# Loads of v split over two DMA queues: partitions 64 to 127 from ScalarE, 0 to 63 from SyncE

## The chip, the cores and the metric

The kernel runs on one core of a Trainium2 chip. The metric is the device time of one execution in microseconds; 225.95 us is the median of three runs of the kernel before. The engines are TensorE (PE, with PEld for its weight loads), VectorE (DVE), ScalarE (ACT), GpSimd (POOL) and SyncE (SP). [...] SP does no arithmetic here; it issues DMAs. [...]

## What is computed

x is 2048 x 512 in bfloat16. It is normalized per row; the result xn feeds two branches, which are multiplied and added to x:

```python
xn = _layernorm(x, axis=-1)
s = _A_ref(xn, A_wqkv, A_wo)          # local dilated attention, 32 heads of 16
g = _silu(_B_ref(xn, B_w_gate, B_w_up, B_w_down))   # (gelu(xn@w_gate) * (xn@w_up)) @ w_down
return x + s * g
```

In the attention, position i sees the eight positions i, i-2, ..., i-14 (W = 8, dilation 2):

```python
idx = pos[:, None] - off[None, :]     # off = 0, 2, ..., 14
kg = k[:, :, idx_c, :].reshape(B, H, S, W, Dh)
vg = v[:, :, idx_c, :].reshape(B, H, S, W, Dh)
logits = jnp.einsum("bhsd,bhswd->bhsw", q, kg) * scale
attn = _softmax(jnp.where(mask, logits, -1e9), axis=-1)
o = jnp.einsum("bhsw,bhswd->bhsd", attn, vg)
```

## The kernel before

The 2048 positions are worked in four blocks of 512 (j = 0 to 3). For each block TensorE does, in this order: 14 GLU steps (`glu`: four matmuls for g_ps with w_gate, four for u_ps with w_up, L261), then the q, k and v projections of the next block (`qkv`, L261), then `down` for four tiles of 128 positions (14 matmuls each into y_ps, L477), with `sums` after the first of them, then `divide` and four times `finish` (four matmuls into s_ps, L493). The last block has no next one, and its `sums` stands at GLU step 12. All these PSUM tiles (g_ps, u_ps, qkv_ps, y_ps, s_ps, the softmax denominators and, for j > 0, the logits) rotate through one pool of four banks, `mm`; a tile waits until the one four before it has been read. In a GLU step ScalarE reads both banks: Gelu of g_ps to ge (L465), a copy of u_ps to u (L467). VectorE multiplies them to h (L469); ge and u have three buffers each.

The attention lies mostly on VectorE, in a layout in which partition 32 w + h holds head h at window offset w modulo 4. `qk_products` multiplies q with shifted k (pk, L332), TensorE sums over the head dimension into L_ps (L352), ScalarE takes the exponential E (L360). `av_product` (L404) and `av_pair` (L420, L428) multiply E with v_arr, TensorE sums into o_ps (L440), and `divide` multiplies with the reciprocal denominators rb into oT (L452), which s_ps reads.

v_arr has 128 partitions x 16 x 520 elements: four groups of 32 partitions, one per window offset wl = 0 to 3, each a shifted copy of the same v. The shift is made by a trip through DRAM: the projected v goes from vst to the DRAM tile vT (L290), and `load_v` (L306) reads it four times with offsets 2 apart, one DMA of 520 KB for each wl. v_arr has a single buffer, shared (tag "va") with pk4, the products of the upper four window positions of the next block: v of block j + 1 can be loaded only when the logits of j + 1 have been read from pk4.

The schedule is written out by hand: `at(key, fn)` hangs a function before a numbered step, `run` calls it there. Every DMA of the kernel before is issued from SP, in program order. At GLU step 0 of block 0 the order on SP is: one transpose of xn (L253), four loads of v, three more transposes, then w_down (L116), w_o (L119) and the rest of x (L88). For the later blocks `sums(j)` ends with: exponentials of block j + 1 on ScalarE; the reciprocals stored to DRAM (rs_d, L389) and read back spread over the partitions (rb, four DMAs, L395), then the four loads of v for j + 1. The one instruction that waits for v on the compute side is the first av_product of a block: GLU step 9 of block 0, GLU step 0 of the others.

On ScalarE the two exponentials in `sums` stand between two table loads: to Exp before (L533), back to Silu (L485) after them for the remaining y_ps tiles.

Of the kernel before, what the change touches and what calls it, by code (L numbers as in the profile page):

```python
# [18 lines left out]
WL = 4  # L19
# [9 lines left out]
def kernel(  # L29
# [13 lines left out]
    nc = tc.nc  # L43
# [225 lines left out]
    st = [dict(pk={}, pv={}, vst={}) for _ in range(NJ)]  # L269
# [27 lines left out]
        project(ps[:, 0, :], wqkv_sb, fo * P, j)  # L297
        copy_out(j, fo, ps[:])

    def load_v(j, wls=range(WL)):  # L300

        if wls[0] == 0:
            st[j]["va"] = vap.tile([P, DH, VW], BF16, name="v_arr", tag="va")
        va = st[j]["va"]
        for wl in wls:
            nc.sync.dma_start(  # L306
                out=va[H * wl : H * (wl + 1), :, :],
                in_=bass.AP(
                    tensor=vT.tensor,
                    offset=PAD + j * TQ - WL * DIL - DIL * wl,  # L310
                    ap=[[SV * DH, H], [SV, DH], [1, VW]],
                ),
            )
# [25 lines left out]
    def logits(j):  # L339
        if j == 0:  # L340
            nc.scalar.preload_act_table(AF.Exp)
            quad = att.tile([P, NC, TQ], F32, name="L_ps", tag="quad")
            L = [quad[:, wh, :] for wh in range(WH)]
        else:
            L = [mm.tile([P, TQ], F32, name="L_ps", tag="mm")[:] for _ in range(WH)]

        Eb = st[j]["Eb"] = ep.tile([P, WH, TQ], BF16, name="E")
        E = st[j]["E"] = Eb[:, ::-1, :]
        for wh in range(WH):
            for c in range(NC):  # L350
                for wl in range(WL):
                    nc.tensor.matmul(  # L352
                        L[wh][H * wl : H * (wl + 1), :],
                        lhsT=dsum[:, c, :],
                        rhs=st[j]["pk"][WL * wh + wl][:, c, :],
                        start=(c == 0),
                        stop=(c == NC - 1),
                    )
        for wh in range(WH):
            nc.scalar.activation(out=E[:, wh, :], in_=L[wh], func=AF.Exp, scale=SCALE)  # L360
        if j == 0:
            for w in range(1, W):
                wh, wl = divmod(w, WL)
                nc.gpsimd.memset(E[H * wl : H * (wl + 1), wh, 0 : w * DIL], 0.0)

    def denominators(j):

        E = st[j]["E"]
        den = mm.tile([P, P], F32, name="den_ps", tag="mm")
        for wh in range(WH):  # L370
            for q in range(4):
                nc.tensor.matmul(  # L372
                    den[H * q : H * (q + 1), :],
                    lhsT=hsum[:],
                    rhs=E[:, wh, q * P : (q + 1) * P],
                    start=(wh == 0),
                    stop=(wh == WH - 1),
                )
        st[j]["den"] = den

    def reciprocals(j):
        den = st[j]["den"]
        rs = sm2.tile([P, P], BF16, name="rs")
        with nc.allow_low_precision(reason="as the softmax of the reference"):
            nc.vector.reciprocal(out=rs[:], in_=den[:])
        st[j]["rs"] = rs

    def store_reciprocals(j):
        nc.sync.dma_start(out=rs_d[j][:, :], in_=st[j]["rs"][:])  # L389

    def spread_reciprocals(j):

        rb = op.tile([P, TQ], BF16, name="rb")
        for i in range(WL):
            nc.sync.dma_start(  # L395
                out=rb[H * i : H * (i + 1), :].rearrange("h (q i) -> h q i", q=4),
                in_=rs_d[j].rearrange("(q h) i -> h q i", h=H),
            )
        st[j]["rb"] = rb
# [32 lines left out]
    def av_sums(j):  # L432

        o = att.tile([P, NC, TQ], F32, name="o_ps", tag="quad")
        for g in range(NC):
            pv = st[j]["pv"]
            pvs = [pv[g]] if g in pv else [pv[g, wh] for wh in range(WH)]
            for n, p in enumerate(pvs):
                for i in range(4):
                    nc.tensor.matmul(  # L440
                        o[H * i : H * (i + 1), g, :],
                        lhsT=hsum[:],
                        rhs=p[:, i, :],
                        start=(n == 0),
                        stop=(n == len(pvs) - 1),
                    )
        st[j]["o"] = o
# [61 lines left out]
    def at(key, fn, *args):  # L509
        side.setdefault(key, []).append((fn, args))  # L510
# [19 lines left out]
    def sums(j):  # L530

        if j + 1 < NJ:
            nc.scalar.preload_act_table(AF.Exp)  # L533
        denominators(j)
        av_sums(j)
        if j + 1 < NJ:
            logits(j + 1)
        reciprocals(j)
        store_reciprocals(j)
        spread_reciprocals(j)  # L540
        if j + 1 < NJ:
            load_v(j + 1)

    for j in range(1, NJ):
        at(("qkv", j, 2), k_halo, j)
# [9 lines left out]
        for i, fc in enumerate(whole):  # L555
            at(("glu", j, fc), av_product, j, npair + i // 2, i % 2)
    at(("glu", NJ - 1, 12), sums, NJ - 1)


# [70 lines left out]
    for n, fo in enumerate((0, 2, 4, 6, 8, 10)):  # L630
# [5 lines left out]
                project(ps[:, i, i0 : i0 + w], wqkv_sb, (fo + i) * P, 0, HQ + i0, w)  # L636
        copy_out(0, fo, ps[:], HQ, HQ, 2)
    at(("glu", 0, 0), transpose_by_dma, TPQ)
    at(("glu", 0, 0), load_v, 0)
    for t in range(TPQ + 1, 2 * TPQ):  # L640
        at(("glu", 0, 0), transpose_by_dma, t)
    at(("glu", 0, 0), load_late_weights)
# [2 lines left out]
    for j in range(NJ):  # L645
        for fc in range(NF):
            run("glu", j, fc)
            glu(j, fc)
        if j + 1 < NJ:

            for i, fo in enumerate((0, 1, 4, 5, 2, 3, 6, 7, 8, 9, 10, 11)):
                run("qkv", j + 1, i)
                qkv(j + 1, fo)
            full = slice(0, D)
            sl = []
            for tt in range(TPQ):
                run("down", j, tt)
                sl.append(down(j, tt, full))
                if tt == 0:
                    sums(j)  # L660
            divide(j)
            for tt in range(TPQ):
                finish(j, tt, full, sl[tt])
        else:
            full, half = slice(0, D), (slice(0, D - P), slice(D - P, D))
            sl = [down(j, tt, full) for tt in range(TPQ - 1)]
            divide(j)
            finish(j, 0, full, sl[0])
            finish(j, 1, full, sl[1])
            finish(j, 2, full, sl[2])  # L670
            sl3 = down(j, 3, half[0])
            finish(j, 3, half[0], sl3)
            sl3 = down(j, 3, half[1])
            finish(j, 3, half[1], sl3)
# [28 lines left out]
```

The softmax here doesn't subtract the row's maximum and nothing guards it: scores larger than these inputs give would overflow.

## Time and profile before

| | |
|---|---|
| median of three runs | 225.95 us (225.94 to 226.25) |
| the profiled execution | 226.18 us |
| its span, first to last instruction | 224.5 us |
| mean granted TensorE clock | 0.999 |
| v_arr loads: issues, length of an issue, issue to landing | 16, 552 / 626 / 746 ns (min, median, max), 5.4 / 8.5 / 12.8 us |
| rb loads: issues, issue to landing | 16, 1.6 / 1.9 / 3.4 us |
| transposes of xn: issues, length of an issue, issue to landing | 12, 1188 / 1286 / 3444 ns, 2.4 / 4.2 / 12.5 us |
| data moved by DMA | 24.89 MB |

How to read it: busy time is the time in which an engine executes; issuing a DMA isn't counted as busy. A wait is idle time of an engine, put down to what released it. SPq rows in the timeline are DMA issues of SP, with the length of the issue, not of the transfer; a row with x4 holds four issues in a row. Matmul ends are modelled, so neighbouring groups overlap by some 0.15 us in the timeline. Some matmul records are missing from the trace.

### The profile page before, as it was taken

To read this page: it belongs to the slowest core of one execution; us is meant where nothing else is said; L and a number is where in the kernel's file an instruction comes from. 1 tells how busy PE (TensorE), PEld (TensorE's weight loads), DVE (VectorE), ACT (ScalarE), POOL (GpSimd) and SP (SyncE) were. 2 spreads that over 40 slices of the span, in tenths; PEclk is the share of its full clock that TensorE was granted. 3 is DMA by queue.
4 is the path that set the end of the run, shared out by engine and by line. 5 is a ranking of instruction groups with operands and counts; after the bars stand their busy time and mean duration, and the time that the engine had idled before them with its cause. 6 is when DMAs were issued, how large, how long until landed. Compare 5 with 4: busy or idle time off the path is not lost.

```text
span 224.5 us, 3548 instructions
## 1 busy us (share of the span) xinstructions
PE 219.3 (98%) x1293; PEld 106.0 (47%) x1314; DVE 172.9 (77%) x295; ACT 130.8 (58%) x207; POOL 21.6 (10%) x67
## 2 busy tenths in 40 slices
PE   8999999999999999999999999999999999999994
PEld 4994444444444444444444444444444444444443
DVE  4688963999984799989984799998944389982452
ACT  4386779667631767676752386767763177666211
POOL 1025981000120000000040000000000000000000
PEclk9999999999999999999999999999999999999999
DMA  6999799972079910000219960000117960001002
GB/s 207 376 402 260 148 198 146 359 212 96 12 152 199 213 23 0 0 3 1 93 41 210 187 164 0 3 0 0 67 41 151 197 147 0 0 0 28 6 23 70
DMA packets 30258, 24.89 MB, mean 111 GB/s; under 512 B 11040, under 2 KB 29728, under 8 KB 30240
## 3 DMA queue, kind: packets, MB, share of 16 engines
q1 hardware_dynamic: 30240, 24.66, 47.1%
q8 instruction: 10, 0.16, 0.3%
q14 instruction: 8, 0.07, 0.1%
HBM read 18.74 MB, written 4.34 MB: 103 GB/s over the span
## 4 chain that ended last, share of the span: by engine, by line
PE 96%; ACT 1%; issue 1%; DVE 0%; ACTq 0%
PE u_ps L261 22%; PE y_ps L477 22%; PE g_ps L261 20%; PE qkv_ps L261 16%; PE s_ps L493 6%; PE L_ps L352 3%; PE o_ps L440 3%; PE qk_ps L576 2%; ACT u L467 1%; PE warm_ps L244 1%; PE v_ps L576 1%; PE qk_ps L567 1%; PE den_ps L372 0%; PE v_ps L567 0%; PE trb L220 0%
## 5 line engine op out<-in xcount | busy, mean ns | idle before, releaser
L261 PE MATMUL u_ps<-xnT,wu_sb 128*128 128x512 bf16 x221 | 57.3, 379 | 0.4
L261 PE MATMUL g_ps<-xnT,wg_sb 128*128 128x512 bf16 x217 | 56.3, 379 | 0.1
L477 PE MATMUL y_ps<-wd_sb,h 128*128 128x512 bf16 (+2 forms) x234 | 49.5, 366 | 0.2
L467 ACT ACTIVATE u<-u_ps 128x512 bf16<-128x512 f32 x56 | 33.5, 599 | 14.8 <-PE u_ps L261 14.8
L465 ACT ACTIVATE ge<-g_ps 128x512 bf16<-128x512 f32 x56 | 33.5, 598 | 11.9 <-PE g_ps L261 8.9
L332 DVE TENSOR_TENSOR pk<-q_sb,k_sb 128x1024 bf16<-128x1024 bf16 (+1 forms) x56 | 38.9, 761 | 1.7 <-ACT k_sb L285 1.7
L261 PE MATMUL qkv_ps<-xnT,wqkv_sb 128*128 128x512 bf16 (+2 forms) x197 | 36.8, 344 | 0.2
L477 PEld LDWEIGHTS <-h 128*128 128x128 bf16 x238 | 22.6, 98 | 26.5 <-issue 1.3
L261 PEld LDWEIGHTS <-wu_sb 128*128 128x128 bf16 x224 | 21.9, 98 | 26.4
L261 PEld LDWEIGHTS <-wg_sb 128*128 128x128 bf16 x224 | 21.7, 98 | 26.6 <-issue 0.8
L404 DVE TENSOR_TENSOR pv<-E,v_arr 128x2048 bf16<-128x2048 bf16 x22 | 26.7, 1220 | 7.4 <-DMA v_arr<-vT 7.4
L485 ACT ACTIVATE sl<-y_ps 128x512 bf16<-128x512 f32 (+2 forms) x17 | 9.7, 572 | 32.7 <-PE y_ps L477 31.6
L469 DVE TENSOR_TENSOR h<-ge,u 128x512 bf16<-128x512 bf16 x56 | 23.1, 419 | 5.9 <-ACT u L467 5.8
L261 PEld LDWEIGHTS <-wqkv_sb 128*128 128x128 bf16 x200 | 18.9, 98 | 17.4
L501 DVE TENSOR_TENSOR m<-s_ps,sl 128x512 bf16<-128x512 f32 (+2 forms) x17 | 11.1, 655 | 18.4 <-PE s_ps L493 13.5
L420 DVE TENSOR_TENSOR two<-E,v_arr 128x1024 f32<-128x1024 bf16 x20 | 24.4, 1218 | 0.0
L204 POOL TENSOR_TENSOR rstd<-rstd,mhalf 128x1 f32<-128x1 f32 x12 | 7.0, 583 | 90.3 <-DVE rstd L201 90.3
L452 DVE TENSOR_TENSOR oT<-o_ps,rb 128x1024 bf16<-128x1024 f32 x8 | 9.4, 1217 | 7.7 <-DMA rb<-rs_d 7.7
L493 PE MATMUL s_ps<-wo_sb,oT 128*128 128x512 bf16 (+2 forms) x64 | 14.6, 366 | 0.2
L428 DVE TENSOR_TENSOR pv<-two 128x512 bf16<-128x512 f32 x20 | 13.8, 692 | 0.7
L465 ACT ACT_TABLE_LOAD x4 | 5.1, 1283 | 11.3 <-PE g_ps L261 11.3
L285 ACT ACTIVATE vst<-qkv_ps 128x512 bf16<-128x512 f32 x14 | 8.4, 597 | 3.7 <-PE qkv_ps L261 3.7
(65 smaller groups left out, 145.2 us busy)
## 6 DMA issues: line engine op xcount, KB each, us to landing
v_arr<-vT SPq DMA_DIRECT2D x16, 520.0 KB, 8.5
vT<-vst SPq DMA_DIRECT2D x8, 256.0 KB, 2.4
out_dram<-o_t SPq DMA_DIRECT2D x15, 128.0 KB, 3.4
wg_sb<-in_B_w_gate_dram SPq DMA_DIRECT2D x2, 896.0 KB, 9.9
wu_sb<-in_B_w_up_dram SPq DMA_DIRECT2D x2, 896.0 KB, 11.2
wd_sb<-in_B_w_down_dram SPq DMA_DIRECT2D x1, 1792.0 KB, 11.6
wqkv_sb<-in_A_wqkv_dram SPq DMA_DIRECT2D x4, 384.0 KB, 4.4
x_sb<-in_A_x_dram SPq DMA_DIRECT2D x3, 512.0 KB, 7.8
```

Source lines behind the costliest of these rows:

```text
L261: nc.tensor.matmul(ps, lhsT=w[:, dk, lo : lo + P], rhs=xnT[j][:, dk, i0 : i0 + n], start=(dk == 0), stop=(dk == NC - 1),)
L332: nc.vector.tensor_tensor(out=st[j]["pk"][w][:, c0 : c0 + n, :], in0=st[j]["q"][:, c0 : c0 + n, :], in1=k_sb[j][:, c0 : c0 + n, off : off ...
L404: nc.vector.tensor_tensor(out=pv[:], in0=st[j]["E"][:, wh, :].unsqueeze(1).to_broadcast([P, 4, TQ]), in1=st[j]["va"][:, 4 * g : 4 * g + 4, ...
L420: nc.vector.tensor_tensor(out=two[:], in0=st[j]["Eb"][:], in1=bass.AP(tensor=v.tensor, offset=v.offset, ap=[v.ap[0], [WL * DIL, WH], [1, T ...
L428: nc.vector.tensor_tensor(out=st[j]["pv"][g][:, d, :], in0=two[:, 0, :], in1=two[:, 1, :], op=ALU.add)
L465: nc.scalar.activation(out=ge[:], in_=g_ps[:], func=AF.Gelu_apprx_tanh)
L467: nc.scalar.activation(out=u[:], in_=u_ps[:], func=AF.Copy)
L469: nc.vector.tensor_tensor(out=h[:], in0=ge[:], in1=u[:], op=ALU.mult)
L477: nc.tensor.matmul(y[:], lhsT=st[j][fc][:, tt * P : (tt + 1) * P], rhs=wd_sb[:, fc, cols], start=(fc == 0), stop=(fc == NF - 1),)
L485: nc.scalar.activation(out=sl[:], in_=y[:], func=AF.Silu)
L493: nc.tensor.matmul(s[:], lhsT=st[j]["oT"][:, g, tt * P : (tt + 1) * P], rhs=wo_sb[:, g, cols], start=(g == 0), stop=(g == NC - 1),)
L501: nc.vector.tensor_tensor(out=m[:], in0=s[:], in1=sl[:], op=ALU.mult)
```

## The change

`load_v` takes the groups wl and the queue from its caller. In `sums` the groups 0 and 1 (partitions 0 to 63) are issued from SP as before, behind rb; the groups 2 and 3 (64 to 127) from ScalarE, where they stand behind the two exponentials and ahead of the Silu table load. For block 0 the groups 0 and 1 stay at GLU step 0 on SP, between the first transpose and the other three; the groups 2 and 3 are issued from ScalarE at GLU step 4, behind the u copy of step 3 and ahead of the Gelu of step 4. The order of all other instructions on every engine is kept. The first av_product of a block waits for all four loads, as before.

```diff
-    def load_v(j, wls=range(WL)):
-
-        if wls[0] == 0:
+    def load_v(j, wls, queue):
+
+        if "va" not in st[j]:
             st[j]["va"] = vap.tile([P, DH, VW], BF16, name="v_arr", tag="va")
         va = st[j]["va"]
         for wl in wls:
-            nc.sync.dma_start(
+            queue.dma_start(
                 out=va[H * wl : H * (wl + 1), :, :],
...
         if j + 1 < NJ:
-            load_v(j + 1)
+
+            load_v(j + 1, (0, 1), nc.sync)
+            load_v(j + 1, (2, 3), nc.scalar)
...
     at(("glu", 0, 0), transpose_by_dma, TPQ)
-    at(("glu", 0, 0), load_v, 0)
+    at(("glu", 0, 0), load_v, 0, (0, 1), nc.sync)
+    at(("glu", 0, 4), load_v, 0, (2, 3), nc.scalar)
     for t in range(TPQ + 1, 2 * TPQ):
         at(("glu", 0, 0), transpose_by_dma, t)
```

## The prediction

> **What bounds the kernel now.** I read the page's busy times first, then its chain, then the waits of all engines, then the timeline where v is loaded. Busy times and the chain's share by engine:
>
> ```profile
> PE 219.3 (98%) x1293; PEld 106.0 (47%) x1314; DVE 172.9 (77%) x295; ACT 130.8 (58%) x207; POOL 21.6 (10%) x67
> ...
> PE 96%; ACT 1%; issue 1%; DVE 0%; ACTq 0%
> ```
>
> TensorE is busy 219.3 of 224.5 us and makes up 96% of the chain. A share over the whole span can hide gaps, so I cut the run at its stage borders (each row: the stretch, its length, then busy time of PE, PEld, DVE, ACT, POOL, then clock, DMA share, GB/s):
>
> ```profile
> 17.10:53.40 36.30, 36.09 (x189) 16.26 (x191) 30.32 (x46) 27.10 (x44) 14.35 (x47) 1.00 0.96 202
> 53.40:72.90 19.50, 19.25 (x143) 8.80 (x145) 15.15 (x32) 8.03 (x10) 2.63 (x5) 1.00 0.63 131
> 72.90:126.30 53.40, 53.14 (x293) 24.13 (x296) 46.05 (x78) 32.28 (x50) 2.63 (x5) 1.00 0.36 72
> 126.30:179.70 53.40, 53.14 (x293) 24.13 (x296) 41.06 (x62) 32.29 (x50) 0.00 (x0) 1.00 0.36 75
> 179.70:221.40 41.70, 41.45 (x235) 19.61 (x237) 28.31 (x43) 21.48 (x35) 0.00 (x0) 1.00 0.13 33
> ```
>
> From 17.10 to 221.40 TensorE is idle for 0.21 + 0.25 + 0.26 + 0.26 + 0.25 = 1.23 us of 204.3. The waits that carry v and its neighbour rb are real, but they are VectorE's (total, times, longest):
>
> ```profile
> DVE oT L452 <- DMA rb<-rs_d: 7.7, 3, 5.3
> DVE pv L404 <- DMA v_arr<-vT: 7.4, 4, 3.7
> ```
>
> VectorE's 7.4 us for v leave no hole on TensorE: they are absorbed. Even the chain's 1% ACT (u L467) is no wait: at 27.30 the timeline shows three of a g_ps group's four matmuls, so one record is missing and the chain steps aside; the groups keep their 0.86 us spacing.
>
> Stage 0, where the first v is loaded (start, length, what):
>
> ```profile
> 22.57 2.71 SPq L306 DMA_DIRECT2D v_arr<-vT  x4
> ...
> 24.11 0.60 ACT L467 ACTIVATE u<-u_ps 128x512 bf16<-128x512 f32 x1 [0.33 <-PE u_ps L261]
> ...
> 24.91 0.60 ACT L465 ACTIVATE ge<-g_ps 128x512 bf16<-128x512 f32 x1 [0.21 <-PE g_ps L261]
> ...
> 25.33 8.57 SPq L253 DMA_TRANSPOSE xnT<-xn  x3
> ```
>
> And the same place for j = 1, after the second softmax:
>
> ```profile
> 60.34 0.60 ACT L360 ACTIVATE E<-L_ps 128x512 bf16<-128x512 f32 x1 [0.22 <-PE L_ps L352]
> 60.40 1.75 SPq L395 DMA_DIRECT2D rb<-rs_d  x4
> ...
> 60.95 1.28 ACT L485 ACT_TABLE_LOAD   x1
> ...
> 62.31 2.65 SPq L306 DMA_DIRECT2D v_arr<-vT  x4
> ...
> 63.45 0.60 ACT L485 ACTIVATE sl<-y_ps 128x512 bf16<-128x512 f32 x1 [1.21 <-PE y_ps L477]
> ...
> 64.08 2.35 DVE L452 TENSOR_TENSOR oT<-o_ps,rb 128x1024 bf16<-128x1024 f32 x2
> ...
> 69.30 3.62 PE L493 MATMUL s_ps<-wo_sb,oT 128*128 128x512 bf16 x15
> ```
>
> The reader should see ScalarE with 1.21 us to spare before its next y_ps, and oT ready at 66.43, 2.87 us before s_ps needs it.
>
> [...] from 64 to 69 us, while v lands, the DMA share is 1.05 at 208 GB/s, so the engines, not the queue, are full. [...] three transposes behind v took 8.57 us, three at 75.17 took 3.81.
>
> **The change, part by part.** Eight of 16 v loads leave SP, 0.626 us each (median of the L306 rows), so 1.25 us per stage. The same eight go to ScalarE, two per stage.
>
> *Stage 0.* The two issues come after u of GLU step 3 (ends 24.71). Behind them wait ge and u of step 4, and thus h(4) on VectorE. TensorE wants the PSUM bank that ge(4) frees (four banks, two per step) for g of step 6 at 27.30. ge takes 0.60, so the two issues may take 27.30 - 0.60 - 24.71 = 2.0 us for nothing. On SP the two loads that stay end near 22.57 + 1.35 = 23.9, and the three transposes, whose inputs are long there, follow at once instead of at 25.33: they meet ScalarE's issues. [...] 0.5 left of the first transpose (23.95 + 1.27 = 25.22), 0.63 for the first v, 1.27 for the second transpose, 0.63 for the second v: 3.0 us, to 27.75. ge(4) ends at 28.35, 1.05 us after 27.30, and TensorE stands for these 1.05 us. Bounds: 1.1 us (2 x 0.552, no waiting; less still if ScalarE issues while u runs), which costs 0; and each issue behind a transpose as slow as those behind four v loads (2.86): 2 x 2.86 + 1.25 = 7.0, a stall of 5.0. I take 3.0: [...] with two loads outstanding rather than four the transposes should take their quiet length. The delay isn't paid twice: u(4) ends at 28.95, its bank is wanted at 28.17 + 1.05, and ScalarE recovers, using 1.20 of each 1.73 us. On VectorE, which was ahead with pk, pk of w = 7 ends near 33.3 instead of 31.49; the logits that read it start at 32.6 + 1.05 and take the w below 4 first. Hidden.
>
> *v for stage 0.* The half on ScalarE starts 1 to 3 us later than now, and SP's transposes and w_down can overtake it. 2.1 MB at 190 to 200 GB/s still needs about 11 us, so v is complete near 37, as now (pv at 37.54). It may be 3.3 us late: h(9) ends 39.11, 1.56 before ge(12) at 40.67, which ends 1.79 before its bank is wanted at 43.06. I take 0; at 4 us late it would be 0.7.
>
> *Stages 1 to 3.* The issues stand after the second E (ends 60.94) and before the Silu table load. Queued behind: table load, three sl. Cost 1.25 us, 2.5 with turns, against 1.21 us of idle before sl: sl starts up to 1.3 us late. Its bank is wanted again only by the second s_ps, past 69.3: nothing. The waits attached are v stores and old loads, all landed (stores issued by 54.6, landing 2.4). All four loads are in flight by about 63.6 rather than 64.96: v at most 1.3 us earlier, so pv's waits (1.50, 1.26, 0.93 us for j = 1, 2, 3) shrink, worth 0. The next transpose is also issued 1.25 us earlier, beside v; should v end 1 us later instead, h(0) slips and ge(3) behind it, but ge(3) (78.99 to 79.59) frees a bank wanted at 81.4: nothing.
>
> *rb.* v stood behind rb; now two v loads enter beside rb's second to fourth. Slack of oT before s_ps: 2.87 (69.30 - 66.43), 2.58 (122.72 - 120.14), 3.26 us (176.15 - 172.89). Delay, low end 0. High end: two issues of 0.63 between rb's issues, 1.25; and three rb loads of 128 rows over 16 engines = 24 rows per engine, each behind one v row (1040 B at 190 GB/s / 16 = 88 ns), 2.1; together 3.4, so 0.5 + 0.8 + 0.1 = 1.4 us of stall in all. I take half of both, 1.7: hidden.
>
> *Start and end.* No v load stands before 22 us or after 172, so head and tail stay. [...]
>
> Sum: 1.05, all from stage 0. The profiled execution took 226.18 us, 1.68 around its span of 224.5, so its like would take 227.2; it lies 0.23 above the median of the runs, 225.95, against which the sum gives 227.0. Since turns can fall a little kinder (ScalarE may issue before u has ended), I say 226.9.
>
> **Rivals.**
> *N, not slower: the issues overlap.* Place: the same two issues of stage 0. If they take 0.63 to 1.0 each beside SP's transposes, ge(4) ends by 27.3 and TensorE never sees them: 226.0. It decides up to 2.0 us for both. For it: four v issues in a row took 0.68 each in this very traffic[...]. Against: [...] SP issuing at just that time. Chance 0.36.
> *A2, worse: the transposes stay slow* and hold ScalarE behind them: 5 to 7 us, a stall of 3 to 5, 229 to 231. For it: 2.86 us each now. Against: half the v loads ahead. 0.09.
> *B, rb comes late in the three later stages,* with or without stage 0's stall: 1.4 at the high end, 227.4. For it: v goes in beside rb, and rb's four issues took 2.66 for j = 2 on their own. Against: all of both parts must add. 0.08.
> *C, faster: v sooner lets VectorE run ahead.* If 7.4 us were on the path it would be 218.5, but TensorE's idle from 17 us on is 1.23 in all. Half of that: 225.3. 0.04.
> *D, the split does nothing for v,* [...] True or not, TensorE doesn't wait for v; the cases above stand.
> *E, a cost around the span or one not listed:* 226.6, 0.04.
>
> **How the numbers follow.** Forecast 0.39, N 0.36, A2 0.09, B 0.08, C 0.04, E 0.04. A measurement here can tell 0.2%, 0.45 us. Faster 0.04, same 0.36, slower 0.60. The forecast's own range is 226.4 to 228.0 (issues of 2.5 to 4 us). N pulls the low end to 225.7; at 228.6 A2 is left out above: 225.7 to 228.6.
>
> **What would show it.** Right: ScalarE's v issues of stage 0 last over 1 us, a hole on TensorE before g of step 6, the time otherwise stage for stage as before, pv's waits for v shorter with no gain. N: those issues at 0.63, PE idle still 0.2 to 0.3 in each stretch. B: s_ps waiting for oT. Wrong altogether: any time below 225.5, or a hole elsewhere.

## The result, and the profile after

| | before | after |
|---|---|---|
| median (lowest to highest) | 226.12 us, 6 runs on the same chip | 239.15 us (238.57 to 241.44), 6 runs |
| ratio, 95% interval | | 1.0586 (1.0536 to 1.0636) |
| profiled execution, its span | 226.18, 224.5 us | 240.8, 239.1 us |
| mean granted TensorE clock in it | 0.999 | 0.979 |

The change costs 13 us. The forecast was 226.9, and no rival went above 231. Here and below medians are over all runs of a kernel, ratios over those within 1.5% of its fastest. First the page of the kernel after: busy times, the granted clock in 40 slices, the two DMA queues (packets, MB, share of 16 engines; q1 is SP's, q10 ScalarE's) and the shares of the engines in the chain of work that ended last.

```profile
PE 225.5 (94%) x1293; PEld 106.6 (45%) x1314; DVE 173.5 (73%) x295; ACT 130.3 (54%) x207; POOL 20.9 (9%) x67
...
PEclk9999999999997999999999799999999989999999
...
q1 hardware_dynamic: 26016, 20.40, 34.3%
q10 hardware_dynamic: 4224, 4.26, 9.4%
...
PE 55%; DVE 21%; DMA 14%; issue 4%; SPq 2%; ACT 1%; ACTq 0%; DVEq 0%
```

The second queue is real: q10 moves 4.26 MB, eight loads of 0.53 MB. TensorE made up 96% of the chain; it makes up 55% now, and 14% are DMA. Such a share says where to look and not how much is lost: in a later experiment (e1) it is 41% and the loss is under 1 us. The clock has three dips that were not there. TensorE is also 6.2 us longer busy with the same 1293 matmuls, as a lower clock would make it.

Next the same stretches that the prediction cut out (length, then busy PE, PEld, DVE, ACT, POOL, then clock, DMA share, GB/s):

```profile
17.10:53.40 36.30, 36.09 (x189) 16.21 (x191) 28.11 (x42) 26.67 (x44) 13.70 (x47) 1.00 0.96 202
53.40:72.90 19.50, 16.91 (x129) 7.30 (x129) 14.96 (x31) 8.03 (x10) 2.63 (x5) 1.00 0.67 138
```

The first stretch holds the stage where the prediction put its whole loss. PE is busy 36.09 us in it, as before. The loss begins in the second, around 70 us. Where GLU starts tells the rest: blocks 1, 2 and 3 began at 72.75, 126.17 and 179.60; they begin at 78.54, 136.44 and 194.21. So 5.8, 4.5 and 4.3 us are lost between GLU of one block and GLU of the next, 14.6 in all, the whole difference of the two spans (the profiled execution is 1.65 us above the median). After 194.21 nothing is lost.

The waits of all engines that carry it (total, times, longest):

```profile
DVE oT L452 <- DMA rb<-rs_d: 21.8, 4, 10.6
...
DVE pv L404 <- DMA v_arr<-vT: 5.9, 1, 5.9
...
PE s_ps L493 <- DVE oT L452: 4.9, 6, 1.5
...
PE s_ps L493 <- DVE m L501: 2.6, 3, 0.9
```

VectorE waits 21.8 us for rb instead of 7.7, and the wait is now passed on: TensorE stands before s_ps for oT, twice in each of the three blocks, and three times for m, the product of s_ps and sl (Silu of y_ps) on VectorE (L501), which no s_ps did before. The timeline of the end of block 0 shows it in order (start, length, what; in brackets the idle time and what ended it):

```profile
61.13 0.33 SPq L389 DMA_DIRECT2D rs_d<-rs  x1
...
61.21 1.24 ACTq L306 DMA_DIRECT2D v_arr<-vT  x2
...
62.60 1.81 SPq L395 DMA_DIRECT2D rb<-rs_d  x4
...
70.63 2.35 DVE L452 TENSOR_TENSOR oT<-o_ps,rb 128x1024 bf16<-128x1024 f32 x2 [4.26 <-DMA rb<-rs_d]
71.91 0.60 PE L493 MATMUL s_ps<-wo_sb,oT 128*128 128x512 bf16 x2 [1.53 <-DVE oT L452]
73.05 0.60 PE L493 MATMUL s_ps<-wo_sb,oT 128*128 128x512 bf16 x2 [0.53 <-DVE oT L452]
...
74.50 2.29 PE L493 MATMUL s_ps<-wo_sb,oT 128*128 128x512 bf16 x5 [0.85 <-DVE m L501]
```

From the store of rs (the reciprocals) to the first load of rb, which reads it back, SP needs 1.5 us, since the store must have landed (1.4 to 1.6 us). ScalarE has nothing of the kind to wait for and issues its two v loads into that gap. What was behind rb in the program is ahead of it now. All four rb loads of this block land 6.5 to 7.0 us after their issue (before: 1.6 to 1.9).

The 5.8 us of this block can be added up. y_ps ends at 70.38, 1.1 later than the s_ps of before began (69.30): mostly a backlog from further up, treated below (the part of y_ps behind the sums began at 61.16 instead of 60.22). Then 1.53 and 0.53 for oT, 0.85 for m, and the rest, 1.8, is slow matmuls. That is read from the weight loads that go with them (same columns):

```profile
74.89 0.15 PEld L493 LDWEIGHTS <-oT 128*128 128x128 bf16 x1 [0.28 <-issue]
75.31 0.15 PEld L493 LDWEIGHTS <-oT 128*128 128x128 bf16 x1 [0.28 <-issue]
75.74 0.15 PEld L493 LDWEIGHTS <-oT 128*128 128x128 bf16 x1 [0.28 <-issue]
```

They start 0.42 us apart, where 0.215 is usual in this kernel (four matmuls of a group in 0.86). The granted clock is 0.50 from 74.06 to 77.47 us, and 1.00 just before and after.

What lands how late depends on what was issued ahead, and block 2 shows it singly. The issues, and then two narrow stretches of them (ns per issue, first and last start; us from issue to landing):

```profile
177.18 1.81 SPq L395 DMA_DIRECT2D rb<-rs_d  x4
...
177.69 1.23 ACTq L306 DMA_DIRECT2D v_arr<-vT  x2
```

```profile
L395 SPq DMA_DIRECT2D rb<-rs_d x1: 423/423/423, 177.6 to 177.6; - x1
...
DMA to landing us min/median/max: 1.7/1.7/1.7
```

```profile
L395 SPq DMA_DIRECT2D rb<-rs_d x2: 428/455/482, 178.0 to 178.5; - x2
...
DMA to landing us min/median/max: 4.4/5.9/7.4
```

ScalarE's two v loads start at 177.7 and 178.3. The rb loads issued ahead of both (177.2, 177.6) land after 1.6 and 1.7 us, the one between them (178.0) after 4.4, the one behind both (178.5) after 7.4. So each v load issued ahead adds 2.7 to 3.0 us. 0.53 MB at the 200 GB/s of this traffic (201 from 62.6 to 66.6 us in block 0) takes 2.7: rb lands as if the v loads ahead of it were moved first.

What the queues moved shows how strictly that holds (packets, MB, share of 16 engines). In block 0, from 62.6 to 66.6 us, with all four rb loads issued by 64.4, and in block 2, from 179.0 to 181.0:

```profile
q10 hardware_dynamic: 789, 0.80, 102.9%
```

```profile
q10 hardware_dynamic: 373, 0.39, 84.1%
q1 hardware_dynamic: 140, 0.03, 8.3%
```

In block 0 SP's queue moves nothing for 4 us while v is moved. In block 2 most of the rb load between the two v loads goes through among the packets of the first v, and only its last few packets come late. oT needs the whole of it, so the landing counts.

### The profile page after: what moved, and what is told of

Same layout as the page of the kernel before. It is cut to its first block, busy times and chain, and to the rows that moved or that the text cites. A ratio compares the mean times of both kernels' runs of the same rounds, so it can differ in the third digit from the quotient of the medians.

```text
span 239.1 us, 3551 instructions
## 1 busy us (share of the span) xinstructions
PE 225.5 (94%) x1293; PEld 106.6 (45%) x1314; DVE 173.5 (73%) x295; ACT 130.3 (54%) x207; POOL 20.9 (9%) x67
## 3 DMA queue, kind: packets, MB, share of 16 engines
q10 hardware_dynamic: 4224, 4.26, 9.4%
## 4 chain that ended last, share of the span: by engine, by line
PE 55%; DVE 21%; DMA 14%; issue 4%; SPq 2%; ACT 1%; ACTq 0%; DVEq 0%
PE u_ps L261 17%; PE g_ps L261 15%; DVE pk L332 12%; PE s_ps L493 7%; DMA rb<-rs_d 6%; DMA v_arr<-vT 6%; PE qkv_ps L261 5%; PE y_ps L477 5%; DVE pv L404 3%; DVE oT L452 3%; DMA rs_d<-rs 2%; SPq L395 2%; PE qk_ps L578 1%; DVE rs L385 1%; DVE m L501 1%
## 5 line engine op out<-in xcount | busy, mean ns | idle before, releaser
L493 PE MATMUL s_ps<-wo_sb,oT 128*128 128x512 bf16 (+2 forms) x64 | 19.8, 443 | 8.2 <-DVE oT L452 4.9
L452 DVE TENSOR_TENSOR oT<-o_ps,rb 128x1024 bf16<-128x1024 f32 x8 | 9.4, 1219 | 21.8 <-DMA rb<-rs_d 21.8
L501 DVE TENSOR_TENSOR m<-s_ps,sl 128x512 bf16<-128x512 f32 (+2 forms) x17 | 11.2, 657 | 14.8 <-PE s_ps L493 9.6
L493 PEld LDWEIGHTS <-oT 128*128 128x128 bf16 x68 | 7.1, 114 | 20.4 <-issue 9.7
## 6 DMA issues: line engine op xcount, KB each, us to landing
wd_sb<-in_B_w_down_dram SPq DMA_DIRECT2D x1, 1792.0 KB, 17.8
```

What stands on the lines that cost most here:

```text
L452: nc.vector.tensor_tensor(out=oT[:, g : g + 2, :], in0=st[j]["o"][:, g : g + 2, :], in1=st[j]["rb"][:].unsqueeze(1).to_broadcast([P, 2, TQ ...
L493: nc.tensor.matmul(s[:], lhsT=st[j]["oT"][:, g, tt * P : (tt + 1) * P], rhs=wo_sb[:, g, cols], start=(g == 0), stop=(g == NC - 1),)
L501: nc.vector.tensor_tensor(out=m[:], in0=s[:], in1=sl[:], op=ALU.mult)
```

## The experiments

The main theory after the result: rb, though small and in another queue, lands only when the v loads that were issued before it are about done, and all else follows from that. Its rivals, with the letters that the expectations use: S, the loss starts with block 0's split; R, the DMA engines serve the two queues in turn, row by row, and two queues rather than the order are what costs; P, ScalarE's queue is preferred. Medians of the kernel before in these comparisons: 226.23 to 226.29 us. "Block 0 on SP" means the lines

```diff
-    at(("glu", 0, 0), load_v, 0, (0, 1), nc.sync)
-    at(("glu", 0, 4), load_v, 0, (2, 3), nc.scalar)
+    at(("glu", 0, 0), load_v, 0, range(WL), nc.sync)
```

All diffs are against the changed kernel if nothing else is said.

**One half of the change at a time.** e1_first_only splits in block 0 alone:

```diff
-            load_v(j + 1, (0, 1), nc.sync)
-            load_v(j + 1, (2, 3), nc.scalar)
+            load_v(j + 1, range(WL), nc.sync)
```

> Block 0 as in the change (half of v from ScalarE at GLU step 4), the later blocks as before (all v from SP behind rb). Theory T (in the later blocks rb is held up behind ScalarE's v loads, oT comes late and TensorE stands before s_ps): rb lands in about 2 us again and 10 to 12 of the 13 us are gone; what is left is v of block 0 landing 2.2 us late, which VectorE carries to the first softmax: 226.5 to 227.5 us. Theory S (the late first v puts VectorE behind, and that is carried on through every block): 236 us or more.

e2_sums_only has block 0 on SP and splits in the later blocks.

> The other half of the change alone: block 0 as before, in the later blocks half of v from ScalarE ahead of rb. T: rb lands 5 to 7 us after its issue in these blocks, TensorE waits for oT three times; 237 to 238.5 us. S: v of block 0 is on time again, so about 226.5 us.

| | median us | ratio (95%) | rb, us from issue to landing |
|---|---|---|---|
| e1_first_only | 227.02 | 1.0030 (1.0011 to 1.0049) | 1.6, 1.8, 3.5 (lowest, median, highest) |
| e2_sums_only | 235.35 | 1.0376 (1.0329 to 1.0422) | first of each block 1.7 to 1.9, slowest 7.0 to 7.3 |

S falls as the main cause: block 0's half costs 0.8 us, the later blocks' half 9.1 (235.35 us, under the 237 to 238.5 expected). Their sum, 9.9, is not 13.0. With block 0's half, rs and so rb are later (rs stored at 61.13 rather than 59.39) and TensorE waits longer at 70 us; the clock dips in three blocks of the profiled execution instead of one.

**Order or queue.** e4_one_queue has everything on SP, v of block 0 as before, and two v loads of the later blocks put where ScalarE's went, between the store of rs and rb:

```diff
         store_reciprocals(j)
+        if j + 1 < NJ:
+            load_v(j + 1, (2, 3), nc.sync)
         spread_reciprocals(j)
...
-            load_v(j + 1, (2, 3), nc.scalar)
```

> All v from SP, none from ScalarE, block 0 as before, but in the later blocks two of the four loads are issued ahead of rb in the same queue. rb then waits in line behind 1.04 MB at about 190 GB/s, 5.5 us, so it lands 6 to 7 us after its issue. If the two queues of the change gave rb no share at all (T in its strict form), time and landing are those of the run with ScalarE's loads ahead of rb, 237 to 238.5 us. If the engines did alternate between the queues row by row (rival R), this run is clearly slower than that one, by 2 us or more in each of three blocks.

e6_rb_on_act turns the roles round: block 0 on SP, all four v loads on SP right behind the store of rs, and rb of blocks 0 to 2 from ScalarE. The two engines then issue side by side, so that the first rb load of a block has at most one v load ahead of it and the last has three or four:

```diff
-        spread_reciprocals(j)
...
-            load_v(j + 1, (0, 1), nc.sync)
-            load_v(j + 1, (2, 3), nc.scalar)
+            load_v(j + 1, range(WL), nc.sync)
+        spread_reciprocals(j, nc.scalar if j + 1 < NJ else nc.sync)
```

> Mirrored: block 0 as before; in the later blocks all four v loads go out from SP right behind the store of the reciprocals, and rb is issued from ScalarE. Which queue is ahead is exchanged. T (whatever was issued first is served first, whichever queue): rb again lands 5 us or more after its issue, behind two to four v loads, 235 us or more. Rival P (the engines serve ScalarE's queue before SP's): rb lands in 2 to 3 us, time 226 to 227.5. Rival R (row by row in turn): rb lands within 4 us, time under 228.

Measured: e4 236.98 us, 1.0395 (1.0374 to 1.0416), in two pairs: 235.19 and 235.21 us with a mean clock of 0.993, 238.75 and 238.82 with 0.978; e6 239.25 us, 1.0554 (1.0515 to 1.0594). The waits for rb and the landings of rb, first of e4, then of e6:

```profile
DVE oT L452 <- DMA rb<-rs_d: 19.0, 3, 11.4
...
DMA to landing us min/median/max: 2.5/6.6/7.0
```

```profile
DVE oT L452 <- DMA rb<-rs_d: 20.6, 3, 13.1
...
DMA to landing us min/median/max: 1.7/5.2/9.0
```

One queue, in e4, gives the loss of e2 (235.2 in the faster pair beside 235.35) and the landings of block 0 of the kernel after (6.1 to 7.0 us beside 6.5 to 7.0). In e6 rb is in the queue that P prefers and alone in it, and is the latest of all: in each block its slowest load lands 8.3 to 9.0 us after issue. R, row by row, and P fall. Whichever queue it stood in, rb landed when about all the bytes issued before it had been moved.

**Dose and place.** e5_one_load gives ScalarE one v load of the later blocks instead of two; block 0 on SP:

```diff
-            load_v(j + 1, (0, 1), nc.sync)
-            load_v(j + 1, (2, 3), nc.scalar)
+            load_v(j + 1, (0, 1, 2), nc.sync)
+            load_v(j + 1, (3,), nc.scalar)
```

> Dose: block 0 as before; in the later blocks ScalarE issues one load of v (wl = 3) ahead of rb instead of two, SP the other three behind rb. If rb waits for all v data that were issued ahead of it (T), half the bytes give half the delay: 0.52 MB at 190 GB/s, 2.7 us, rb lands in 4 to 5 us, just about the slack of 2.6 to 3.3 us that oT has: 226 to 228.5 us, far from half of the loss. A delay that doesn't go with the bytes (a fixed cost of a second queue): 230 us or more.

e3_late_act keeps the split but issues ScalarE's two loads later, before the third y_ps step, when rb is under way; block 0 on SP:

```diff
-            load_v(j + 1, (2, 3), nc.scalar)
...
+        at(("down", j - 1, 2), load_v, j, (2, 3), nc.scalar)
```

> As the run before, but ScalarE issues its two v loads later, behind the Silu table load and the second y_ps, some 3 us on, when rb has landed. ScalarE still issues the same two loads in each block. T: rb lands in about 2 us, oT is on time: 226.0 to 226.5 us. Rival L (it is the issue on ScalarE itself, its wait or its place between the table loads, that costs): still over 230 us.

e5: 226.26 us, 0.9998 (0.9988 to 1.0007). Its rb:

```profile
DMA to landing us min/median/max: 1.7/3.4/5.3
```

The last rb load of a block lands after 4.6 to 5.3 us. oT of the three blocks ends at 69.4, 123.1 and 176.3, and s_ps begins at 69.7, 123.2 and 176.6: just in time. One load ahead is within the slack, two are beyond it. That is the dose the main theory asks for.

e3: 227.86 us, 1.0071 (1.0044 to 1.0098). rb lands after 1.6 to 3.0 us and the loss is nearly gone, so rival L falls, but not quite: 226.0 to 226.5 was expected. The timeline of its s_ps hints at why: the group of block 0 takes 3.96 us,

```profile
69.30 3.96 PE L493 MATMUL s_ps<-wo_sb,oT 128*128 128x512 bf16 x15
```

where it took 3.62. In this build the third and fourth s_ps of a block get the PSUM banks of the first and second, and so wait for m; before, all four found banks that ScalarE's sl had freed. (The extra time lies before these two, but the pauses are too short for the profile to name what ended them; e12 below is the test.) 0.34 a block is 1.0 us, against the measured 1.6.

**The bank waits.** The mm pool's choice of a bank for s_ps moves with the order of instructions. In the kernel after, the second s_ps of a block waits for m of the first, 0.85 us three times. A control was to give the four s_ps a four-bank tile of their own, in e8_quad (the change) and e9_late_quad (e3):

```diff
-        s = mm.tile([P, n], F32, name="s_ps", tag="mm")
+        if tt == 0:
+            st[j]["s4"] = att.tile([P, TPQ, TQ], F32, name="s_ps", tag="quad")
+        s = st[j]["s4"][:, tt, cols.start : cols.stop]
```

> The changed kernel, but s_ps takes the four PSUM banks that o_ps has just left, not the pool of four that rotates. In the build of the change the second s_ps of a block waits for m of the first (VectorE), where it waited for a sl of ScalarE before. If that wait costs what the trace shows before the fifth s_ps matmul (about 0.85 us in each of three blocks), 236 to 238 us; if the whole loss is rb's lateness, 239 us as the changed kernel.

> ScalarE's two loads behind the second y_ps (after rb), block 0 as before, and s_ps in the banks that o_ps left. If what the late version lost (227.86 us) is the shift of PSUM banks (its third and fourth s_ps wait for m of the first and second), this is 226.0 to 226.5 us; if ScalarE's issues themselves cost, 227.5 us or more.

It is no control: 252.59 us for e8 (one run at 247.8, three from 252.04 to 253.43, so no ratio) and 237.49 for e9, 1.0493 (1.0468 to 1.0519). As slices of one tile, each s_ps waits for the m before it. The waits of e9:

```profile
PE s_ps L495 <- DVE m L503: 9.4, 11, 0.9
```

It still gave a price: rb in time, clock at 1.0, eleven waits of 0.85 us, and the time is 9.6 us above e3.

e10_turn_after and e12_turn_late avoid that by handing out the pool's four banks in strict turn, for the change and for e3 (the first eight tiles as listed, then 0, 3, 1, 2 over and over):

```diff
-    mm = pool("mm", 4, space=bass.MemoryType.PSUM)
+    mm_banks = pool("mm", 1, space=bass.MemoryType.PSUM)
+    class Turn:
+        n = 0
+        first = (0, 1, 2, 3, 0, 3, 0, 3)
+        def tile(self, shape, dt, name, tag):
+            self.n += 1
+            n = self.n - 1
+            k = self.first[n] if n < 8 else (0, 3, 1, 2)[n % 4]
+            return mm_banks.tile(shape, dt, name=name, tag=f"mm{k}")
+    mm = Turn()
```

> The changed kernel with the four PSUM banks of the mm pool taken in strict turn, so that no s_ps waits for m of the one before (in the build of the change the second s_ps of each block does). If that wait is a part of the loss (about 0.85 us in each of three blocks, by the trace), 235.5 to 237 us against 239.15; if it isn't, 239 us.

> The late version (ScalarE's two loads behind the second y_ps, block 0 as before) with the banks in strict turn. If the 1.6 us that the late version lost were its waits of s_ps for m, 226.0 to 226.6 us, no different from before; if ScalarE's issues or v's lateness cost, still 227.5 us or more.

e10: 232.94 us, 1.0309 (1.0266 to 1.0353). e12: 226.65 us, 1.0017 (1.0005 to 1.0029). In e12 the s_ps group is back at 3.61 us, so the bank waits were most of what e3 had lost; 0.4 us stay unexplained. In e10, which was expected at 235.5 to 237, the waits for m are gone, and the clock's dips with them in the profiled execution and two more; the fourth run, 235.22 us, has a mean clock of 0.993:

```profile
PEclk9999999999999999999999999999999999999999
```

```profile
71.72 0.60 PE L505 MATMUL s_ps<-wo_sb,oT 128*128 128x512 bf16 x2 [1.91 <-DVE oT L464]
72.85 3.19 PE L505 MATMUL s_ps<-wo_sb,oT 128*128 128x512 bf16 x13 [0.53 <-DVE oT L464]
```

TensorE still waits 1.91 and 0.53 us for oT, as the order theory wants, and then runs at a clock of 1.00 (69 to 79 us). e10 is 6.2 us faster than the change, whose waits for m were 3 x 0.85 = 2.55, so some 3.7 are left for the clock. The change's own runs agree: the median of their mean clocks is 0.985 where before it is 1.00, and 1.5% of the 237 us span is an estimated 3.6.

**The clock alone.** e13_line_warm is e4, which has no waits for m, with twelve matmuls on constants put between the products with rb and s_ps; they leave the result alone and fall into the time in which TensorE stands (diff against e4):

```diff
+            warm_up(12, TQ)
```

> The one-queue version (two v loads ahead of rb, 236.98 us) with 12 matmuls of 512 columns on constants put on TensorE before the first s_ps of a block: 2.6 us of work where it stands idle for rb. If the low clock after the stall comes from the idleness, s_ps runs at full clock and some 1 us comes back in each of three blocks, 232 to 235 us; if the clock has another cause, or its loss is nothing, 237 us or more.

e13: 234.21 us, 1.0357 (1.034 to 1.0375), all four runs from 233.99 to 234.82 with a mean clock of 1.00. From 69 to 79 us, e4 (its profiled execution is one of the pair at 238.8) and then e13 (columns as above):

```profile
69.00:79.00 10.00, 7.84 (x29) 3.07 (x29) 7.59 (x11) 1.96 (x3) 0.00 (x0) 0.83 0.61 120
```

```profile
69.00:79.00 10.00, 9.94 (x47) 4.43 (x47) 7.96 (x12) 3.27 (x5) 0.00 (x0) 1.00 0.73 139
```

rb is as late in both (VectorE's longest wait for it is 11.4 us in e4 and 11.6 in e13); with the idle time filled, the mean clock is 1.00 in every run. So the low clock goes with the idle time here and not with rb's lateness. How much comes back depends on what it is set against: 1.0 us against the faster pair of e4, where the two intervals still touch, 4.6 against the slower. The pairs themselves give the price. The profile of e4 has three dips of 3.41 us at half clock, which make its mean of 0.978; a mean of 0.993 is that of one dip, as in the profile of e2. So two dips more cost an estimated 3.6 us, the distance of the pairs, 1.8 each.

**v of block 0.** In e1 and in the change the first v is complete later. With fewer v issues ahead of them the transposes and then w_down come forward on SP and run beside v: in the change w_down is issued at 28.68 instead of 33.95 and lands after 17.8 us instead of 11.6, and from 29 to 38 us SP's queue moves 0.45 MB beside 1.05 MB of ScalarE's. e11_first_wd_late is e1 with the late weights held back to GLU step 7:

```diff
-    at(("glu", 0, 0), load_late_weights)
+    at(("glu", 0, 7), nc.vector.memset, wd_sb[:, 0, 0:2], 0.0)
+    at(("glu", 0, 7), load_late_weights)
...
-        at(("glu", 0, 0), load_x, j * TPQ, TPQ)
+        at(("glu", 0, 7), load_x, j * TPQ, TPQ)
```

> Block 0 of the change alone (227.02 us), but w_down, w_o and the rest of x are issued from GLU step 7 on (a tiny memset of w_down on VectorE holds them back), as late as in the kernel before. If v of block 0 came 2 us late because w_down shares the DMA engines with ScalarE's half of v, v is on time at 37 to 38 us and the time 226.0 to 226.6; if splitting v in itself delays it, v stays near 40 us and the time near 227.

e11: 226.70 us, 1.0031 (1.0015 to 1.0048), the same as e1. The first pv starts at 38.79 us, between before (37.54) and the change (39.76), and the time does not follow. Inconclusive: w_down goes out at 31.54, not yet as late as before, v is only partly back, and the held weights can cost something themselves. That the 0.8 us of e1 is v's lateness carried by VectorE to the reciprocals of block 0 fits the timeline, and isn't shown.

No version beats the kernel before. e5, the best, equals it.

## Why the prediction was wrong

**The bound: right.** TensorE had no gaps to give, and no version was faster than before. Rival C (faster) had nothing to take.

**Stage 0's turns of ScalarE's and SP's issues, the whole of the forecast's 1.05 us: fell.** The turns were an estimate of the author's, which no trace had shown. The timeline there in the kernel after:

```profile
24.29 1.37 ACTq L306 DMA_DIRECT2D v_arr<-vT  x2
24.43 4.21 SPq L253 DMA_TRANSPOSE xnT<-xn  x3
...
25.76 0.60 ACT L465 ACTIVATE ge<-g_ps 128x512 bf16<-128x512 f32 x1 [1.04 <-PE u_ps L261]
```

The two issues took 1.37 us in place of 3.0, although SP issued transposes beside them nearly all the time, 1.4 us each. ScalarE also began them while u was still running. ge(4) ended at 26.36, 0.94 before the 27.30 that was allowed. The two issues show no wait for SP's: their 657 and 674 ns are within the 552 to 746 of the loads before. Rival N had this step right.

**rb, the step that failed.** Rival B named the place and the mechanism, rb late in the later stages, but priced its data part at 2.1 us at most ("24 rows per engine, each behind one v row") and its chance at 0.08; the sum then took half of the 3.4 us high end, 1.7, as "hidden". That price assumed engines that alternate, row by row, between the queues, which no trace had shown. Measured: 2.7 to 3.0 us for each v load issued ahead, 5 to 6 for both. Against a slack of 2.6 to 3.3 us that is the difference between 1.4 us of stall and the 4.9 that s_ps waited for oT. The other part, 1.25 us for v's issues between rb's, was 0: rb's four issues take 1.81 us, 1.75 before, except for 2.70 in block 1, where before had 2.66. The bound "each behind one v row" was not a bound. The high end was rb behind all of v's bytes that are issued before it, 2 x 0.53 MB at 200 GB/s = 5.3 us, and the trace of before showed that price: its four v loads, issued 0.63 us apart, land up to 12.8 us after issue. Where v enters was right for blocks 1 and 2, beside rb's later loads (177.7 against 177.2 for the first rb load in block 2). In block 0 it was not: there rs comes late (stored at 61.13, where it was 59.39 in e2 and 58.92 before), and both v loads go out in the 1.5 us in which SP waits for rs to be stored, ahead of all four rb loads.

Packets in this trace are nearly rows: the eight v loads of ScalarE's queue have 4096 rows and make 4224 packets, on average 33 for each of 16 engines and load. In block 0 an engine moves an average of 789 / 16 = 49 of v's while rb waits; in block 2, from 179.0 to 181.0, 140 packets of SP's queue go in beside 373 of v's. What decides between the two, no run tells. The two halves on two queues did not bring v sooner in block 0 (first pv at 39.76 instead of 37.54), and the price of 13 us is more than that nothing is gained.

**v of block 0: half right.** "Complete near 37" became 39.76, within the 3.3 us that had been allowed without a stall of GLU, and GLU did not stall. But VectorE kept the delay until the reciprocals: rs is stored at 61.13 instead of 58.92, and about 1 us of it reaches TensorE by the end of block 0. "I take 0" should have been about 1.

**Banks: missed.** "s_ps ... nothing" took the banks of before for granted. In the build of the change s_ps gets others, three waits of 0.85 us.

**The clock: missed.** No step of the sum asked what a stall does to the matmuls after it. Together with the waits for m it is worth 6.2 us (e10), nearly as much as the 6.7 that rb and v's lateness leave in e10.

**Start and end: right,** nothing lost before 17 us or after the last GLU begins.

The 13.0 us, then: 6.7 with all bank waits gone (e10 over before: rb's lateness and block 0's backlog), 2.55 of waits for m, and some 3.7 of low clock, which is what is left over and near the 3.6 that the mean clocks give.

## What to carry to other kernels

Before moving a DMA to a second queue, ask which small transfer on the path it can now overtake, above all one that must first wait for a store; price that small transfer behind all bytes issued ahead of it, on either queue (here 2.7 to 3.0 us for each load of 0.53 MB), and compare with its slack. A stall that is found is not the end of the sum: add what the matmuls behind it may lose to the clock (here an estimated 1.8 us for each dip), and look for waits that a moved instruction has changed elsewhere, such as those for a PSUM bank.

## What was not expected of the hardware

Loads on two queues of different engines landed nearly as if they stood in one line in order of issue: rb behind one v load landed after 4.0 to 5.3 us (but after 1.7 when it was issued within 0.15 us of it, in e6), behind two after 6.1 to 7.4, behind three or four after 8.3 to 9.0, in the same queue (e4) or in the other, and with the roles exchanged (e6).

TensorE's granted clock fell to 0.50 for 3.41 us, three times in the kernel after: from 74.06, 132.09 and 190.11 us. Around the first of these starts TensorE had pauses of 1.53, 0.53 and 0.85 us within 4.1 us, with matmuls between them, and around the third 0.78, 0.52 and 0.85; with 1.91 and 0.53 (e10), or 1.10, 0.52 and 0.85 (block 0 of e2), the clock did not fall. The longest pause doesn't decide, 1.53 and 0.78 with a dip and 1.91 and 1.10 without, and neither does their sum, 2.91 and 2.15 with and 2.44 and 2.47 without.

How long TensorE was busy in the 3.4 us before doesn't settle it either. First the stretches right before two dips of the kernel after, then two stretches of e2, the first without a dip behind it and the second with one, and last a stretch of e10, without a dip (columns as above, PE busy first):

```profile
70.65:74.06 3.41, 1.21 (x4) 0.33 (x5) 2.64 (x3) 0.37 (x1) 0.00 (x0) 1.00 1.16 189
...
186.70:190.11 3.41, 1.38 (x5) 0.42 (x6) 2.60 (x4) 0.51 (x1) 0.00 (x0) 1.00 1.08 183
```

```profile
68.62:72.04 3.42, 1.80 (x9) 0.51 (x7) 2.35 (x2) 0.60 (x1) 0.00 (x0) 1.00 1.13 196
...
181.26:184.68 3.42, 1.72 (x7) 0.33 (x6) 2.47 (x3) 0.60 (x1) 0.00 (x0) 1.00 1.13 193
```

```profile
69.00:72.40 3.40, 1.42 (x6) 0.31 (x4) 1.96 (x2) 0.60 (x1) 0.00 (x0) 1.00 1.13 195
```

With a dip behind them: 1.21, 1.38 and 1.72 us. Without: 1.80 and 1.42, and 1.49 of mostly smaller matmuls at the end of the kernel after (234.49 to 237.90). What decides isn't shown. By the mean clock the same kernel came with one dip and with three: the two pairs of e4 have 235.2 us at a mean clock of 0.993 and 238.8 at 0.978. With twelve filler matmuls in such a stall (e13) the mean clock was 1.00 in all four runs.
